# First attention layer reordered: second and third step exchanged, gMLP weight loads held until the last x rows are transposed, one row transpose per attention tile, three row blocks' output projections a step later

## The chip, the cores and the metric

One core of one Trainium2 chip. The metric is the device time of one execution in microseconds (us). The span that a profile shows is some 1.75 us shorter than the time of the same run.

## The reference, cut to what matters

```python
def reference(A_x, A_wqkv, A_wo, B_x, B_w_in, B_w_sp, B_b_sp, B_w_out):
    x = A_x                                            # (1, 2048, 576), bf16
    x = x + _A_ref(_layernorm(x), A_wqkv, A_wo)        # 32 heads of 18; each query sees 8 keys,
    x = x + _B_ref(_layernorm(x), B_w_in, B_w_sp, ...) #   2 positions apart
    x = x + _A_ref(_layernorm(x), A_wqkv, A_wo)        # B is a gMLP: w_in (576 x 4608), gelu,
    x = x + _B_ref(_layernorm(x), B_w_in, B_w_sp, ...) #   w_sp (2048 x 2048) over the rows, w_out
    return x
```

The change touches the first line of these four alone. The first attention layer takes about 135 of 1190 us.

## The kernel before

An attention layer goes through NT = 19 tiles of 112 queries, each in two steps: step 2t has heads 0 to 15 of tile t, step 2t+1 heads 16 to 31. A step is 16 logit matmuls (`L_mm`, TensorE), two exponentials (`EXP`, ScalarE) and 16 small matmuls with v (`PV`, TensorE), whose result VectorE divides by its sum (`rec`, `o_t`). All other work of the layer hangs in a table at a step number: projections of q and k (`PG`) and v (`VW`), the output projection of 128 rows (`WO`), the load of their residual (`XO`), the store of the new x (`XST`), its normalisation, and the transpose of the normalised row block for the next layer (`LN_T`). Transposes of attention rows (`o_t` to `oT`) and of row blocks are DMAs that SyncE's queue (SPq) issues in program order, together with the loads and stores.

```python
        def XO(i):                                     # two row blocks at once, on SPq
            if i % 2 == 0:
                xo = ...
                self.dma(xo[:], x_prev[i * P:(i + 2) * P, :]..., eng=nc.sync)
        def WO(i, hh):
            ...
            for c in range(5):
                nc.tensor.matmul(pw[:, 0:288], lhsT=oT[:, c, r0:r0 + P], rhs=wo_sb[:, c, hh * 288:(hh + 1) * 288], ...)
            nc.vector.tensor_tensor(out=st["x"][:, hs], in0=pw[:, 0:288], in1=st["xo"][:, hs], op=ALU.add)
        ...
        for t in range(nvw, NT):                       # nvw = 9 in the first layer
            for hh in range(2):
                if li == 0 and t == nvw:
                    at(13 * hh, VW, t, hh, True)
                else:
                    at(2 * t - 2 + hh, VW, t, hh, 2 * t - 2 + hh >= PG_END and hh == 0)
        for i in range(NS):                            # 16 row blocks
            t = -(-(i + 1) * P // QT) - 1              # the last tile that block i needs
            s = 2 * t + (6 if li == 0 and t < 10 else 5 if t < NT - 5 else 4 if t < NT - 3 else 3)
            at(s - 5, XO, i)
            at(s, WO, i, 0)
            at(s + 1, WO, i, 1)
            at(s + 1, LN_STATS, i)
            at(s + 2, LN_XN, i)
            at(s + 2, XST, i)
            if i < NS - 1:
                at(max(s + 4, 24 + (5 * i) // 4) if li == 0 else s + 4, LN_T, i)
        if li == 0:
            at(0, self.load_wo, nc.sync)
            for f in reversed(self.load_win2a(nc.gpsimd)):
                at(0, f)
        # [cut: loads of win2b, the first six PG with L_mm(0), EXP(0) and the four window fills]
        for s in range(NST):                           # NST = 38
            if s + 1 < NST:
                L_mm(s + 1)
                EXP(s + 1)
            PV(s)
            for f, a in table.pop(s, []):
                f(*a)
```

Four PSUM buffers (128 x 512) are shared by all of `PG`, `VW`, `PV` and `WO`. TensorE can start one of these only when VectorE or ScalarE has emptied the buffer of four before.

The softmax here doesn't subtract the row's maximum and nothing guards it: scores larger than these inputs give would overflow.

## Time and profile before

Three runs before the prediction gave 1190.21 us (1190.11 to 1192.29). The profile lines that carry the argument are in the prediction. This table gives what one profiled run of the kernel before shows, in us; a row of it is the start of the first instruction of that kind on TensorE.

| milestone | profile before |
|---|---|
| first PV (step 0) | 49.01 |
| PV of step 14 | 80.95 |
| PV of step 16 to PV of step 22 | 12.24 |
| PV of step 23 to PV of step 24 | 1.86 |
| last PV (step 37) | 129.18 |
| first gMLP matmul that uses the second part of its weights | 133.46 |
| end of the last matmul | 1187.78 |
| tail: from the start of VectorE's last add (1187.81) to the end | 2.99 |
| span | 1190.8 |

### The profile page before, as it was taken

Reading aid. Unit: us, or ns where it says so; the run is one execution under the profiler, and the core shown is the slowest. Engines: PE = TensorE matmul, PEld = TensorE weight load, DVE = VectorE, ACT = ScalarE, POOL = GpSimd, SP = SyncE. Lnnn points to the kernel's source line nnn. Section 1 sums busy time; section 2 is a strip of 40 time slices with the busy share of each in tenths; the row PEclk is TensorE's granted clock in tenths of the full one; section 3 lists DMA queues with packets and bytes.
Section 4 is the critical chain, followed back from the end, with each engine's and each line's share of the span. In section 5 each row is a group of like instructions: output and inputs, shape, how many; then the busy total and the mean of one; then the engine's idle time right before and its main releaser. Section 6 shows DMA issues by size and latency. Waiting matters only on the chain.

```text
span 1190.8 us, 20761 instructions
## 1 busy us (share of the span) xinstructions
PE 1180.2 (99%) x8554; PEld 620.6 (52%) x8554; DVE 547.4 (46%) x1206; ACT 376.6 (32%) x593; POOL 281.5 (24%) x383
## 2 busy tenths in 40 slices
PE   8999999999999999999999999999999999999998
PEld 5567544444444444457755775444444444444677
DVE  8688587333233233245556786753233233233311
ACT  5578677210110110202156786760110110111000
POOL 4768685000000000001153877530000000000000
PEclk9999999999999999999999999999999999999999
DMA  8989992000000000049645999900000000000332
GB/s 195 200 163 199 181 224 65 23 4 9 12 12 12 12 1 11 12 139 291 169 98 117 203 227 196 202 14 9 12 12 1 12 12 12 12 1 28 125 105 73
DMA packets 178104, 101.21 MB, mean 85 GB/s; under 512 B 134336, under 2 KB 159360, under 8 KB 178009
## 3 DMA queue, kind: packets, MB, share of 16 engines
q1 hardware_dynamic: 165144, 78.13, 30.6%
q0 software_dynamic: 6512, 16.00, 5.4%
q10 hardware_dynamic: 6352, 5.75, 1.6%
q8 instruction: 67, 1.10, 0.4%
q14 instruction: 29, 0.23, 0.1%
HBM read 42.39 MB, written 16.53 MB: 49 GB/s over the span
## 4 chain that ended last, share of the span: by engine, by line
PE 94%; DMA 3%; POOL 1%; ACT 0%; issue 0%; SPq 0%; DVE 0%; ACTq 0%; DVEq 0%
PE pg L887 42%; PE pz L869 12%; PE po L941 12%; PE pz L791 11%; PE pp L402 5%; PE pw L494 3%; PE O_ps L457 3%; PE pv L379 3%; PE L_ps L437 2%; DMA oT<-o_t 2%; PE pzs L791 1%; DMA QK<-win2a 1%; POOL QK L77 1%; DMA wqk_sb<-in_A_wqkv_dram 1%; ACT P_sb L446 0%
## 5 line engine op out<-in xcount | busy, mean ns | idle before, releaser
L887 PE MATMUL pg<-Wq,Z 128*128 128x512 bf16 x2304 | 502.8, 379 | 0.0
L887 PEld LDWEIGHTS <-Z 128*128 128x128 bf16 x2304 | 225.3, 98 | 272.0
L891 DVE TENSOR_TENSOR g_tmp<-pg,ln_xn 128x512 f32<-128x512 f32 x144 | 99.6, 692 | 429.2 <-PE pg L887 429.2
L881 ACT ACTIVATE z1T<-pz 128x1024 bf16<-128x1024 f32 x72 | 73.7, 1024 | 513.8 <-PE pz L869 513.6
L77 POOL DMA_DIRECT2D wout<-in_B_w_out_dram x4 | 4.3, 1064 | 604.6 <-PE pg L887 604.6
L941 PE MATMUL po<-wout,Z 128*128 128x288 bf16 x1152 | 141.4, 286 | 0.0
L446 ACT ACTIVATE P_sb<-L_ps 128x896 bf16<-128x896 f32 (+1 forms) x152 | 126.7, 887 | 41.2 <-PE L_ps L437 40.6
L869 PE MATMUL pz<-xnT,w 128*128 128x512 bf16 (+1 forms) x640 | 136.0, 380 | 0.0
L941 PEld LDWEIGHTS <-Z 128*128 128x128 bf16 x1152 | 112.7, 98 | 28.8
L791 PEld LDWEIGHTS <-xnT 128*128 128x128 bf16 (+1 forms) x800 | 66.2, 97 | 81.0 <-issue 23.7
L791 PE MATMUL pz<-win2a,xnT 128*128 128x512 bf16 x384 | 104.8, 380 | 0.0
L892 DVE TENSOR_TENSOR Z<-g_tmp,z1T 128x512 bf16<-128x512 f32 x144 | 99.6, 692 | 9.7
L869 PEld LDWEIGHTS <-w 128*128 128x128 bf16 (+1 forms) x640 | 51.1, 97 | 80.0 <-issue 27.1
L402 PE MATMUL pp<-xnT,wqk_sb 128*128 128x512 bf16 x360 | 83.8, 382 | 0.5 <-DMA wqk_sb<-in_A_wqkv_dram 0.5
L805 ACT ACTIVATE zp<-pz 128x1024 bf16<-128x1024 f32 x64 | 65.5, 1024 | 36.6 <-PE pz L791 32.8
L951 DVE TENSOR_TENSOR x_new<-po,xo 128x288 f32<-128x288 f32 (+1 forms) x64 | 28.8, 455 | 87.6 <-PE po L941 83.5
L791 PE MATMUL pz<-win2b,xnT 128*128 128x512 bf16 (+1 forms) x256 | 65.7, 380 | 0.0
L807 DVE CUSTOM_DVE_ANT_0 Z<-zp 128x1536 bf16<-128x1536 bf16 x32 | 56.6, 1769 | 13.1 <-ACT zp L805 13.0
L77 POOL DMA_DIRECT2D QK<-stg x81 | 50.7, 631 | 36.3 <-DVE stg L371 21.0
L379 PE MATMUL pv<-wv_sb,xnT 128*128 128x288 bf16 (+1 forms) x380 | 55.8, 285 | 0.0
L242 POOL TENSOR_SCALAR ln_xn<-x_new,ln_mv,ln_rstd 128x576 bf16<-128x576 f32 x23 | 52.8, 2294 | 2.0
L402 PEld LDWEIGHTS <-wqk_sb 128*128 128x128 bf16 x360 | 33.2, 98 | 37.2 <-DMA wqk_sb<-in_A_wqkv_dram 1.0
(114 smaller groups left out, 916.9 us busy)
## 6 DMA issues: line engine op xcount, KB each, us to landing
xres<-x_new SPq DMA_DIRECT2D x48, 288.0 KB
xo<-xres SPq DMA_DIRECT2D x32, 288.0 KB
wout<-in_B_w_out_dram POOLq DMA_DIRECT2D x4, 1296.0 KB, 8.5
xo<-xres SPq DMA_DIRECT2D x8, 576.0 KB
w<-in_B_w_in_dram SPq DMA_DIRECT2D x16, 256.0 KB
QK<-stg POOLq DMA_DIRECT2D x53, 72.0 KB, 4.4
QK<-stg SPq DMA_DIRECT2D x41, 72.0 KB
xo<-in_A_x_dram SPq DMA_DIRECT2D x8, 288.0 KB
```

The lines of the kernel that those rows point to most:

```text
L77: return eng.dma_start(out=out, in_=in_)
L379: nc.tensor.matmul(pv[:nk, 0:288], lhsT=self.xnT[:, c, QT * t:QT * t + nk], rhs=wv_sb[:, c, hh * 288:(hh + 1) * 288], start=(c == 0), stop ...
L402: nc.tensor.matmul(pp[:, :], lhsT=w, rhs=self.xnT[:, c, PADL + cc * 512:PADL + (cc + 1) * 512], start=(c == 0), stop=(c == 4))
L446: nc.scalar.activation(out=P_bufs[(2 * s + jp) % 4][:nk, :, :, 0:nq], in_=Lv[:nk, :, :, 0:nq], func=ACT.Exp, scale=scale)
L791: nc.tensor.matmul(pzvs[ci][:, sub * 512:sub * 512 + w], lhsT=self.xnT[r0:r1, c, PADL + i * P:PADL + (i + 1) * P], rhs=win2(c)[r0:r1, c0 + ...
L805: nc.scalar.activation(out=zp[:, c0:c0 + cn], in_=pzvs[ci][:, 0:cn], func=ACT.Gelu_apprx_tanh, accum_out=sums[:, ci:ci + 1])
L869: nc.tensor.matmul(pz1s[q // 2][:, q % 2, :], lhsT=w1[r0:r1, c, sub * P:(sub + 1) * P], rhs=self.xnT[r0:r1, c, PADL + q * 512:PADL + (q + ...
L881: nc.scalar.activation(out=z1T[:, q2 * 512:(q2 + 2) * 512], in_=pz1s[q2 // 2][:, :, :].rearrange("p a b -> p (a b)"), func=ACT.Gelu_apprx_ ...
L887: nc.tensor.matmul(pg[:, :], lhsT=Z[:, jj, i, sub * P:(sub + 1) * P], rhs=Wq[q][:, i, :], start=(i == 0), stop=(i == NS - 1))
L891: nc.vector.tensor_tensor(out=tmp[:], in0=pg[:, :], in1=bsp[:, qs], op=ALU.add)
L892: nc.vector.tensor_tensor(out=uT(jj)[:, sub, qs], in0=tmp[:], in1=z1Ts[jj, sub][:, qs], op=ALU.mult)
L941: nc.tensor.matmul(acc[hh], lhsT=uT(j // 2)[:, j % 2, i * P:(i + 1) * P], rhs=wouts[j // NJH][:, j % NJH, hh * 288:(hh + 1) * 288], start= ...
```

## The change

Its intent is to remove three holes of TensorE in the first attention layer: the wait for the q weights at 14 us, the wait for staged q and k rows at 48 us, and the waits for transposed attention rows near the end of the layer.

```diff
+        parts = dict(k=(D, 512, D + 64), q=(0, D, 0), q0=(0, 256, 0), q1=(256, D - 256, 256), k1=(D + 512, 64, D))
-            self.load_wqk(nc.sync)
+            self.load_wqk(nc.sync, ("k", "q0", "q1", "k1"))
 # [cut]
+        seq = list(range(NST))
+        if li == 0:
+            seq[1:3] = 2, 1
+        pbi = {s: 2 * k_ for k_, s in enumerate(seq)}      # which P_sb buffer a step uses
 # [cut: EXP and PV use pbi[s]; L_mm, EXP and PV are called with seq[s]]
-                xn = stgs[(2 + k_) % NSTG]...
+                xn = stgs[(1 + k_) % NSTG]...
 # [cut: v evacuations of tiles 4 and 5 on ScalarE; VW(9, 0) moved ahead of the loop]
                 if li == 0 and t == nvw:
-                    at(13 * hh, VW, t, hh, True)
+                    if hh == 1:
+                        at(0, VW, t, hh, True)
 # [cut]
-            s = 2 * t + (6 if li == 0 and t < 10 else 5 if ...)
+            s = 2 * t + (7 if li == 0 and 5 <= t <= 7 else 6 if li == 0 and t < 10 else 5 if ...)
 # [cut]
-                at(max(s + 4, 24 + (5 * i) // 4) if li == 0 else s + 4, LN_T, i)
+                at(s + 4 if li > 0 or i > 12 else 19 + 2 * i if i < 8 else 35 + (i - 8) // 2, LN_T, i)
         if li == 0:
+            at(1, self.fill_window_rows, QK, 1, ((4, 0),))     # two of four fills; the others before the loop
+            at(2, self.fill_window_rows, QK, 1, ((4, 1),))
             at(0, self.load_wo, nc.sync)
-            for f in reversed(self.load_win2a(nc.gpsimd)):
-                at(0, f)
+            at(0, lambda: nc.gpsimd.tensor_copy(out=rstds[:, 0:1], in_=self.xnT[:, 0, PADL + S - 1:PADL + S]))
+            w2l = self.load_win2a(nc.gpsimd)
+            for k_ in (3, 5, 4, 2, 1, 0):
+                at(0, w2l[k_])
```

The copy of one element of xnT on GpSimd is the hold: GpSimd issues the weight loads after it, and it waits for the last transposed x rows. `5 <= t <= 7` selects row blocks 4, 5 and 6.

## The prediction

> **What bounds the kernel now.** I read the page first, then the waits of TensorE (PE), then the order of time of PE, VectorE (DVE) and SyncE's DMA queue (SPq) around the holes that the waits named. The page:
>
> ```profile
> span 1190.8 us, 20761 instructions
> PE 1180.2 (99%) x8554; PEld 620.6 (52%) x8554; DVE 547.4 (46%) x1206; ACT 376.6 (32%) x593; POOL 281.5 (24%) x383
> ```
>
> PE is busy 1180.2 of 1190.8 us and carries 94% of the chain that ended last. The change touches only the first attention layer (everything in it hangs on li == 0, or has the old default), adds no matmul and removes none: the order of PE in the changed kernel has the same 17110 rows, with a few groups moved. So the whole prize is the idle and the stretched time of PE in the first 135 us; from there to the end PE is fed by itself, and what is won at 135 us should arrive at the end unchanged. The waits of PE over the whole run:
>
> ```profile
> PE pw L494 <- DMA oT<-o_t: 1.8, 2, 1.2
> PE L_ps L437 <- ACT P_sb L446: 1.6, 5, 0.4
> PE warm L541 <- POOL ident L184: 1.5, 1, 1.5
> PE pt L574 <- DVE ln_xn L567: 1.2, 2, 0.8
> PE L_ps L437 <- DMA QK<-win2a: 0.7, 1, 0.7
> PE pp L402 <- DMA wqk_sb<-in_A_wqkv_dram: 0.5, 1, 0.5
> ```
>
> Columns: total us, times, longest. The rows named DMA (oT, QK, wqk_sb) are what the change aims at: 3.0 us, 0.25% of the run. Three holes, in order of time. First, 0.55 us at 14.47 us before the first q projection, until its weights land. Second, the second logits step (tile 0, heads 16 to 31):
>
> ```profile
> 47.28 0.89 PE L437 MATMUL L_ps<-QK 32*128 32x112 bf16 x15
> 48.86 0.22 PE L437 MATMUL L_ps<-QK 32*128 32x112 bf16 x1 [0.69 <-DMA QK<-win2a]
> 49.01 0.56 PE L457 MATMUL O_ps<-v_ext,P_sb 128*128 128x19 bf16 x16
> ```
>
> Such a group of 16 takes 0.40 us where nothing holds it (57.45 us); here 47.28 to 49.01, 1.73 us, so about 1.3 us are lost, more than the wait counts. Just after it, the chain that ended last shows the same projection group at two speeds:
>
> ```profile
> 51.05 2.14 PE pp L402 x5
> ...
> 54.22 1.09 PE pp L402 x5
> ```
>
> The granted clock is 0.50 in every slice between 50.9 and 53.6 us, 1.00 before 50.5 and after 54. A window of about 3.4 us at half speed follows the hole. Its cost is 1.05 us in that group, about 1.2 us in all. Third, the end of the layer: output projections wait for transposed attention rows.
>
> ```profile
> 125.22 0.79 PE L494 MATMUL pw<-wo_sb,oT 128*128 128x288 bf16 x5 [0.59 <-DMA oT<-o_t]
> ...
> 131.51 1.39 PE L494 MATMUL pw<-wo_sb,oT 128*128 128x288 bf16 x10 [1.23 <-DMA oT<-o_t]
> ```
>
> SPq shows why: it takes some 1.23 us to issue each transpose, in order.
>
> ```profile
> 121.02 1.78 SPq L469 DMA_TRANSPOSE oT<-o_t  x1
> 122.90 1.23 SPq L249 DMA_TRANSPOSE xnT<-stg  x1
> 124.18 0.57 SPq L77 DMA_DIRECT2D xres<-x_new  x1
> 124.84 1.23 SPq L249 DMA_TRANSPOSE xnT<-stg  x1
> 126.17 0.53 SPq L77 DMA_DIRECT2D xo<-in_A_x_dram  x1
> 126.80 1.19 SPq L469 DMA_TRANSPOSE oT<-o_t  x1
> ```
>
> The transpose issued at 126.80 belongs to attention tile 16, whose rows DVE had finished at 125.3 us at the latest (the multiply at 124.85, 0.46 us). It lands 4.57 us after its issue, at 131.4. Two row transposes and one load of the residual stand between it and the one before.
>
> **What the Trainium skill says.** "TensorE: Matmul & The Clock Gate", part 1 (the HAM clock gate): PE's clock falls to half after an idle window of about 3.4 us on a free-running grid, and returns after a busy one. The trace agrees in length and ratio (0.50 for about 3.4 us, 2.14 against 1.09 us); that the free-running phase decides whether it strikes is my reason for not counting on this gain in every run. The same page (table at its top) says that VectorE is strict FIFO; so fills queued ahead of a reciprocal delay it, which matters below. The trace fits: the reciprocal at 49.61 comes after four fills that end at 49.32. "Trainium Kernel Development and Optimization", key constraints: DMAs from SP, ACT and POOL share the same 16 engines. The trace agrees: while POOL's weight loads run, 50 to 55 us, 372 GB/s move, against 143 in the next 5 us.
>
> **The change part by part.**
>
> *Weights of q in two pieces.* Before the first q group, 576+72 = 648 KB had to land after k; now 256+32 = 288 KB. At the 288 to 310 GB/s measured between 5 and 15 us, 360 KB less is about 1.2 us earlier, which covers the 0.55 us. PE is then back to back until 47 us. The two extra issues on SPq (about 0.55 us each) delay later x loads by 1.1 us, but no PE work before 39 us uses those, and DVE has 2.8 us of slack at 34.7. Gain 0.5 us.
>
> *Second and third step exchanged.* PE now has a v projection (moved ahead, 0.61 us), the logits of tile 1 heads 0 to 15 (whose rows are long in place), the first PV (0.42 us) and another v projection (formerly at step 13, 0.61 us) before it needs the late heads. Starting at 47.28 that is about 49.3, past the 48.8 landing: the DMA wait goes. But another takes its place: the two logits buffers are held by the two exponentials, 1.73 us for the pair. Logits of tile 1 end at 48.2, their exponentials at about 50.0, so the exchanged step cannot finish before about 50.2 and the next PV starts at 50.3; before, the PV in that place started at 50.46. Gain 0.2 us there, and one v projection already done. Step 13 loses that projection: its PV-to-PV time was 78.73 to 80.95, 2.22 us; steps 14 to 17, without one, average (88.31-80.95)/4 = 1.84 us, which is ScalarE's floor of two exponentials. Gain 0.38. Together 0.6 us, not 1.3.
>
> *Half-rate window.* The hole before it now holds work, so it should mostly go: 1.2 us in the profiled run. But timed runs before were 1190.11, 1190.21 and 1192.29, the profiled one 1192.6; perhaps the faster ones never had it. I count 0.5 us of the median.
>
> *gMLP weight loads held.* Six loads of 288 KB, issued at 45.99 to 51.06 while the last four x transposes (issued 41.93 to 47.13) are in flight, now wait for these. With the rest ahead of its time by some 0.7 us, the projection at step 1 needs these rows at about 50.2; holding keeps them from being late. They end on POOL about 4 us later, and POOL's first staging copy (56.40 before) is late by about 1 us at most; its columns are wanted only at step 18. Gain 0, as protection.
>
> *Window fills split.* DVE had four fills in a row (4.64 us). Two now come before the first reciprocal, one each after steps 1 and 2. DVE work in these steps is 0.26+0.46+0.69+1.16 = 2.57 us against about 2.0 for PE; four PSUM buffers carry the lag of about 1 to 2 us. Gain 0. Four v evacuations moved to ScalarE fall in its idle stretch (6.94 us before 41.78): 0.
>
> *One row transpose per tile; output projections of rows 4 to 6 one step later.* Row transposes start at step 19 and come every second step; before, from step 24, nearly every step. An attention tile then costs SPq 1.23+1.23+0.57+0.55/2 = 3.3 us, against about 4.3 us for two steps: SPq keeps up. Between the last two attention transposes one row transpose goes (1.2 us), and the residual load that stood last in front of tile 16 comes earlier (up to 0.5 us). Both oT waits (0.59+1.23 = 1.8 us) should shrink to near nothing. Gain 1.5 us.
>
> Sum: 0.5 + 0.6 + 0.5 + 1.5 = 3.1 us; 1190.2 - 3.1 = 1187.1 us.
>
> **Rivals.** (1) *The transposes only move their congestion.* For: DMA is near saturation at 85 to 135 us (SP's queue takes 94.5% of 16 engines), and the attention transpose issued at 90.38 took 9.51 us; DVE waited 1.6 us for it to reuse an output row buffer. Three more row transposes now fall between steps 19 and 23. Against: the residual stores of rows 4 to 6 move later, and SPq idles from 98 to 101.5. If so, the 1.5 us shrink to 0 and the time is about 1188.7. (2) *ScalarE floor or DVE lag eats the exchange.* With nothing from the exchange and 0.5 us lost to the fills, about 1188.2. (3) *The hole, or the half-rate window, was worth more:* the window gone in all runs, 1.2 instead of 0.5, and oT waits fully gone: about 1186.
>
> **Range and chances.** All rivals lie between 1186 and 1189; a slow run as the median could add 2 us. Range 1185.0 to 1189.8. A 2% move is 24 us, and all PE idle of the layer is about 6.5 us, so faster by over 2% is near impossible; slower by 2% would need a new stall of 20 us, and nothing in the order of instructions makes one: 0.005 each, within 2% 0.99.
>
> **What would show it.** Right: no wait of pp on wqk_sb; no wait of L_ps on QK, but the first logits steps waiting on the exponentials; clock 1.00 at 50 to 55 us; no or smaller oT waits at the end, with the last attention transpose issued within 1 us of its rows; first gMLP matmuls some 3 us earlier. Wrong: pp waiting for xnT around 50 us, DVE waiting on oT<-o_t for over 2 us at 90 to 105, or new PE idle at steps 13 to 16.

## The result, and the profile after

Four runs of the changed kernel gave a median of 1192.49 us (1191.05 to 1195.34), beside 1190.28 us for the kernel before (four runs, 1190.11 to 1192.29). The ratio is 1.0018, with a 95% interval of 0.9994 to 1.0041: within 2%, and above the predicted range of 1185.0 to 1189.8. All ratios here are those on record, of fast runs of the same rounds; they are not quite the ratios of the medians, nor of the plain means (e11: 1190.88 over 1191.54 us is 0.9994, where 1.0001 is on record).

The page of the changed kernel: the span is longer by 1.1 us, and TensorE is busy for 0.4 us more (1180.6 after 1180.2), though it does the same 8554 counted instructions.

```profile
span 1191.9 us, 20761 instructions
...
PE 1180.6 (99%) x8554; PEld 620.7 (52%) x8554; DVE 546.0 (46%) x1202; ACT 377.9 (32%) x597; POOL 275.8 (23%) x384
```

The waits of TensorE in the changed kernel (total us, times, longest): the wait on QK is gone, those on oT fell from 1.8 to 0.4, and exponentials took over, 2.5 instead of 1.6. The wait of pp on the q weights is gone, and a wait of pp on xnT has come (at 23.65 us, not near 50 us, where the prediction would have taken it as a sign of being wrong).

```profile
PE L_ps L441 <- ACT P_sb L450: 2.5, 7, 0.4
...
PE pp L402 <- DMA xnT<-ln_xn: 0.7, 1, 0.7
PE pw L498 <- DMA oT<-o_t: 0.4, 1, 0.4
```

TensorE in order of time at the exchanged steps, changed kernel (start, duration, instructions, in brackets the idle time before and what ended it). The logits at 48.18 take 0.40 us, unhindered; the first PV is at 48.51 (49.01 before). The half group at 50.37 waits for an exponential, and the second PV comes 2.16 us after the first.

```profile
48.18 0.40 PE L441 MATMUL L_ps<-QK 32*128 32x112 bf16 x16
48.51 0.57 PE L461 MATMUL O_ps<-v_ext,P_sb 128*128 128x19 bf16 x16
...
50.37 0.37 PE L441 MATMUL L_ps<-QK 32*128 32x112 bf16 x8 [0.34 <-ACT P_sb L450]
50.67 0.56 PE L461 MATMUL O_ps<-v_ext,P_sb 128*128 128x19 bf16 x16
```

So the front of the layer goes roughly as forecast: the PV of step 14 starts at 79.88, 1.07 us before its time in the profile before. But steps 16 to 22 then take 13.17 us instead of 12.24, the last PV is 0.3 us later than before, and the gMLP milestone is only 1.07 us earlier, where some 3 had been forecast. VectorE in the changed kernel shows what is new there: the add of an output projection waits 3.04 us for its residual load `xo`, and the reciprocal behind it, which empties a PSUM buffer, waits with it.

```profile
85.44 0.46 DVE L468 TENSOR_TENSOR o_t<-O_ps,rec 112x288 bf16<-112x288 f32 x1 [0.83 <-DMA oT<-o_t]
...
89.61 0.46 DVE L501 TENSOR_TENSOR x_new<-pw,xo 128x288 f32<-128x288 f32 x1 [3.04 <-DMA xo<-in_A_x_dram]
89.98 0.25 DVE L467 RECIPROCAL rec<-O_ps 112x16 f32<-112x16 f32 x1
```

SyncE's queue in the changed kernel shows why it is late: the load of xo stands behind four staging copies, which take 3.98 us to issue, and goes out at 84.96.

```profile
79.05 1.27 SPq L473 DMA_TRANSPOSE oT<-o_t  x1
80.42 3.98 SPq L77 DMA_DIRECT2D QK<-stg  x4
84.45 0.47 SPq L77 DMA_DIRECT2D xres<-x_new  x1
84.96 0.42 SPq L77 DMA_DIRECT2D xo<-in_A_x_dram  x1
```

Two more things cost time. From 86.3 to 89.7 us, and again at 687 us in the second attention layer, which the change does not touch, the profile shows TensorE at half clock. The windows view of the second one (stretch, its length, busy time and count of PE, PEld, DVE, ACT and POOL, granted clock, DMA share, GB/s):

```profile
687.00:690.40 3.40, 3.40 (x47) 2.03 (x44) 1.17 (x3) 1.64 (x4) 1.33 (x3) 0.50 1.17 267
```

And the tail, from the start of the last add to the end of the program, takes 3.77 us instead of 2.99. (The span is printed to 0.1 us, so a tail is good to 0.05.)

### The profile page after: what moved, and what is told of

It reads as the page before. It is cut to its first block, busy times and chain, and to the rows that moved or that the text cites. A ratio compares the mean times of both kernels' runs of the same rounds, so it can differ in the third digit from the quotient of the medians.

```text
span 1191.9 us, 20761 instructions
## 1 busy us (share of the span) xinstructions
PE 1180.6 (99%) x8554; PEld 620.7 (52%) x8554; DVE 546.0 (46%) x1202; ACT 377.9 (32%) x597; POOL 275.8 (23%) x384
## 3 DMA queue, kind: packets, MB, share of 16 engines
q10 hardware_dynamic: 6352, 5.75, 1.6%
## 4 chain that ended last, share of the span: by engine, by line
PE 96%; DMA 2%; ACT 1%; issue 0%; SPq 0%; DVE 0%; ACTq 0%
PE pg L896 42%; PE pz L878 12%; PE po L950 12%; PE pz L800 11%; PE pp L402 6%; PE pv L379 3%; PE pw L498 3%; PE O_ps L461 3%; PE L_ps L441 2%; PE pzs L800 1%; ACT P_sb L450 1%; DMA wqk_sb<-in_A_wqkv_dram 1%; DMA oT<-o_t 1%; DMA oT<-in_A_x_dram 0%; SPq L77 0%
```

## The experiments

Three candidates were on the table for the missing 3 us: the later output projections of row blocks 4 to 6 (with the late residual load), half-clock windows that strike elsewhere, and the longer end of the program; and a fourth, that the one profile of the kernel before had been a poor base. Milestones of the profiles, in us, in the columns of the table above and three more, PV of step 16 to PV of step 22, PV of step 23 to PV of step 24, and the tail, from the start of VectorE's last add to the end (row "before" is that profile again; "clock 1.0" marks a profiled run whose mean granted clock was 1.0):

| profile | first PV | step 14 | 16 to 22 | 23 to 24 | step 37 | gMLP | end PE | tail | span |
|---|---|---|---|---|---|---|---|---|---|
| before | 49.01 | 80.95 | 12.24 | 1.86 | 129.18 | 133.46 | 1187.78 | 2.99 | 1190.8 |
| e5, before again (clock 1.0) | 48.74 | 79.71 | 12.25 | 1.62 | 127.21 | 131.50 | 1185.84 | 3.03 | 1188.9 |
| e6, before again | 50.39 | 84.75 | 12.24 | 1.62 | 132.64 | 137.38 | 1191.70 | 3.06 | 1194.8 |
| after | 48.51 | 79.88 | 13.17 | 2.06 | 129.50 | 132.39 | 1188.09 | 3.77 | 1191.9 |
| e1, after again (clock 1.0) | 47.48 | 78.85 | 12.93 | 2.06 | 127.68 | 130.56 | 1184.88 | 3.78 | 1188.7 |
| e13, after again | 47.35 | 78.72 | 15.22 | 2.06 | 130.24 | 133.12 | 1187.44 | 3.73 | 1191.2 |
| e16, after again | 47.93 | 79.31 | 13.68 | 2.06 | 128.90 | 131.78 | 1188.52 | 3.74 | 1192.3 |
| e2, projections undone (clock 1.0) | 47.94 | 80.52 | 12.25 | 1.62 | 128.07 | 130.96 | 1185.28 | 3.38 | 1188.7 |
| e3, row transposes undone | 47.55 | 79.27 | 13.00 | 2.07 | 128.18 | 133.40 | 1188.93 | 3.74 | 1192.7 |
| e4, idle matmuls added (clock 1.0) | 47.62 | 78.99 | 14.27 | 2.21 | 129.53 | 132.42 | 1188.44 | 3.72 | 1192.2 |
| e7, residual load earlier | 47.79 | 79.17 | 14.11 | 2.19 | 129.19 | 132.08 | 1187.52 | 3.74 | 1191.3 |
| e8, q in one load | 47.58 | 78.96 | 14.02 | 2.19 | 128.88 | 131.76 | 1186.52 | 3.04 | 1189.6 |
| e9, no exchange | 49.13 | 80.87 | 14.46 | 2.21 | 131.24 | 134.13 | 1188.88 | 3.79 | 1192.7 |
| e10, no hold | 47.25 | 83.10 | 11.82 | 2.17 | 130.82 | 133.70 | 1188.02 | 3.74 | 1191.8 |
| e11, e2 and e8 together (clock 1.0) | 47.24 | 78.61 | 12.24 | 1.61 | 126.16 | 129.04 | 1183.36 | 3.01 | 1186.4 |
| e12, e11 and v projection back | 47.36 | 79.37 | 15.34 | 1.62 | 130.03 | 132.92 | 1187.23 | 3.03 | 1190.3 |
| e14, before and later projections | 48.33 | 79.91 | 13.55 | 2.22 | 129.10 | 132.39 | 1186.70 | 3.06 | 1189.8 |
| e15, e11 again | 47.66 | 79.02 | 14.85 | 1.62 | 129.18 | 132.07 | 1187.79 | 2.97 | 1190.8 |

And the times, each beside the kernel before on the same chip and in the same rounds. A call, in what follows, is one submission of several runs to one chip: e1 to e4; e5 and e6; e7 to e10; e11 to e14; e15 and e16. The last column counts the runs whose mean granted clock was 1.0 as listed, not 0.999 or less.

| run | n | median us | ratio to before, 95% | clock 1.0 |
|---|---|---|---|---|
| after | 4 | 1192.49 | 1.0018 [0.9994, 1.0041] | 0 |
| e1 (after) | 6 | 1191.87 | 1.0001 [0.9982, 1.0019] | 2 |
| e13 (after) | 6 | 1191.22 | 1.0000 [0.9983, 1.0016] | 1 |
| e16 (after) | 6 | 1192.36 | 0.9995 [0.9974, 1.0015] | 0 |
| e5 (before) | 6 | 1192.59 | 1.0005 [0.9982, 1.0027] | 2 |
| e2 | 6 | 1191.63 | 0.9995 [0.9977, 1.0013] | 3 |
| e3 | 6 | 1193.05 | 1.0013 [0.9994, 1.0032] | 1 |
| e4 | 6 | 1194.09 | 1.0014 [0.9998, 1.0030] | 4 |
| e7 | 5 | 1191.77 | 1.0010 [0.9998, 1.0023] | 1 |
| e8 | 5 | 1191.32 | 1.0001 [0.9988, 1.0013] | 1 |
| e9 | 5 | 1194.45 | 1.0024 [1.0011, 1.0038] | 0 |
| e10 | 5 | 1193.67 | 1.0030 [1.0017, 1.0044] | 0 |
| e11 | 6 | 1190.09 | 1.0001 [0.9979, 1.0022] | 3 |
| e12 | 6 | 1191.20 | 1.0003 [0.9982, 1.0024] | 2 |
| e14 | 6 | 1192.48 | 1.0012 [0.9992, 1.0031] | 2 |
| e15 | 6 | 1191.17 | 0.9988 [0.9968, 1.0009] | 2 |

### The two kernels unedited: e1, e13, e16 (after) and e5, e6 (before)

No edit: the same kernels were run several times because single runs of one differ by more than the effect.

> The changed kernel again, unedited. Theory CHANCE (the number of half-rate windows of TensorE differs from run to run by the phase of a free-running grid; the first four runs of the changed kernel were unlucky): median at or below 1190.3, ratio to before 0.998 to 1.000. Theory PLACE (the change thins TensorE's work at attention steps 13 to 16 and so makes a half-rate window there in nearly every run, 1.3 us): median again 1191 to 1194, and the profile again shows a granted clock well under 1.00 between 80 and 95 us. Theory TRANSPOSES (row transposes in steps 19 to 23 slow the chain): waits for oT or o_t longer than in the first profile.

> The kernel before, unedited, submitted as a run to get a second profile of it. Reason: in the call before, five of its eleven runs had a granted clock of 1.0 and took 1189.96 to 1191.44 us, no longer than the changed kernel's runs at 1.0. Theory ATYPICAL (the profile that the prediction was read from was a run with a bad hole at 47 us and a half-rate window after it; in most runs of the kernel before these are smaller or absent, so there was less to win): in this profile, if its clock is 1.0, the second logits group starts its PV before 48.5 us, the first gMLP matmuls with win2b come at 130.5 to 131.5 instead of 133.46, and the waits for oT are under 1 us. Theory GIVEN BACK (the kernel before always has the hole and the waits; the changed kernel wins them in the first layer and loses as much later): the hole at 47 us and the win2b matmuls at 132.5 to 133.5 come again, and the end is no later than the changed kernel's only because later stages are shorter.

> The kernel before once more, one look, for a third profile. ATYPICAL and GIVEN BACK as for the run before it; and the spread of the start of the first gMLP matmuls over three profiles shows how far one profile can be trusted: CHANCE expects it to differ by 1.5 us or more between profiles of the same kernel.

> The changed kernel, unedited, as the partner of the others in this call. PLACE: at most two of six runs at clock 1.0, a window at 80 to 95 us in the profile with a chance of about 5 in 7 (five of seven profiles of kernels with the thinned steps and no filler had it). Median 1191.5 to 1192.5.

> The changed kernel as its partner. GIVEN BACK BY THE LATER PROJECTIONS: steps 16 to 22 take 12.9 us or more (12.93, 13.17 and 15.22 in its three profiles so far), step 24 2.06 us, tail 3.75 us, median 0.5 to 2 us above the run beside it. CHANCE: no difference beyond 0.7 us.

Of what was expected: e1 bore out neither CHANCE (its median is above 1190.3) nor PLACE (its profile has no window at 80 to 95 us). e5 met one of ATYPICAL's three signs (gMLP at 131.50; but its first PV is at 48.74 and its oT wait 1.5 us). e6 met CHANCE, with a spread of 5.9 us. e13 met PLACE (one run at clock 1.0, a window at 90 us), with a median 0.3 us under the range. e16 met what was expected of it, but the intervals of both e15 and e16 hold 1.

The 60 runs of the kernel before in the experiments (e5 and e6 among them) have a mean of 1192.10 us, a median of 1191.72 and a standard deviation of 2.10. The 22 runs of the changed kernel (the first four, e1, e13 and e16) have a mean of 1192.19 and a median of 1192.09. So the change is worth nothing that these runs can see: a mean difference of +0.1 us, with a standard error of about 0.4 (0.27 and 0.34, added in squares). The base of the prediction, 1190.21 us, was a lucky draw of three.

The spread has a visible part. Of the 60 runs before, 24 had a mean clock of 1.0, and those average 1190.30 us; of the 22 runs after, 3 had it (1190.76 us). With different chips and rounds mixed in, 24 of 60 against 3 of 22 speaks for half-clock windows striking the changed kernel more often; the count over all runs, after e14 below, says the same more clearly.

The three profiles of the kernel before differ by 5.9 us at the start of the gMLP (131.50 to 137.38). The one that I predicted from had a half-clock window at 50 us and two oT waits; e5, at full clock, has the hole at 48 us, one oT wait of 1.5 us and no window; e6 has three oT waits (4.0 us in all) and a half-clock window at 76 to 79.5 us, just after the first of them (1.61 us). The waits of TensorE in e5:

```profile
PE L_ps L437 <- ACT P_sb L446: 1.6, 5, 0.4
PE pw L494 <- DMA oT<-o_t: 1.5, 1, 1.5
...
PE L_ps L437 <- DMA QK<-win2a: 0.7, 2, 0.5
```

There is no wait of pp for wqk_sb among them: that one is 0.55 us in the first profile of before, 0.40 in e6, 0 in e5.

e5 and e1 are the two kernels at full clock, so they give the cleanest ledger, worked out from the table. To the PV of step 16 (83.39 in e5, 82.52 in e1) the changed kernel gains 0.87 us; from step 16 to 22 it gives back 0.68; from 22 to 37 it gives back 0.66; at the end of the layer it gains 1.41. The sum, 0.94 us gained at the start of the gMLP (131.50 to 130.56), is still there at TensorE's end (0.96, 1185.84 to 1184.88). Then the tail takes 0.75 us of it back: 0.2 us of span remain.

SyncE's queue in e5, to be held against that of the changed kernel above: here xo is issued at 79.31, ahead of the staging copies.

```profile
77.94 1.26 SPq L469 DMA_TRANSPOSE oT<-o_t  x1
79.31 0.52 SPq L77 DMA_DIRECT2D xo<-in_A_x_dram  x1
79.92 3.10 SPq L77 DMA_DIRECT2D QK<-stg  x4
```

In e1 it goes out at 83.81. VectorE waits 1.36 us for it there, then 1.48 us for an o_t buffer that a late transpose still reads, and TensorE has a wait that no profile of the kernel before has:

```profile
PE pv L379 <- DVE o_t L468: 1.1, 1, 1.1
```

Which of VectorE's two waits holds TensorE? The chain that ended last (start, duration) goes through the transpose in e1:

```profile
84.34 4.55 DMA oT<-o_t
```

and through the load in e16:

```profile
84.63 4.84 DMA xo<-in_A_x_dram
```

It is the load in e13 and e4 too, where TensorE waits 1.83 and 1.14 us for the add that needs it (1.64 in e16), and the transpose in e3 and e14. The two are issued one directly after the other, behind the same four staging copies (83.81 and 84.34 in e1). So what stalls is that place in the queue; the price of the load alone is not separated from that of the transpose.

Steps 16 to 22 took 12.24 to 12.25 us in all three profiles of the kernel before, and 12.93 to 15.22 in all four of the changed one.

### e2: later output projections undone

```diff
-            s = 2 * t + (7 if li == 0 and 5 <= t <= 7 else 6 if li == 0 and t < 10 else ...)
+            s = 2 * t + (6 if li == 0 and t < 10 else ...)
```

> The changed kernel with the output projections of rows 4 to 6 back at their old steps (16 to 21), so step 16 has its projection again and steps 22 and 23 lose it. PLACE: the half-rate window between 80 and 95 us is gone or rarer, and the time falls by about 1.3 us against the changed kernel of the same call; CHANCE: no difference clear of 1 us; TRANSPOSES: no difference, or slower because the stores come a step earlier.

In the profile, steps 16 to 22 are back at 12.25 us and step 23 to 24 at 1.62; no wait for xo is left. The time is 1191.63 us against 1191.87 for e1 of the same call: no difference to be seen. Waits for oT came back instead (0.33 and 0.52 us, at 66 and 72 us), and the gain to step 14 was lost with them (80.52). From step 16 to 37 it takes 43.88 us, against 45.16 in e1 and 43.82 in e5.

### e3: row transposes back in their old places

```diff
-                at(s + 4 if li > 0 or i > 12 else 19 + 2 * i if i < 8 else 35 + (i - 8) // 2, LN_T, i)
+                at(max(s + 4, 24 + (5 * i) // 4) if li == 0 else s + 4, LN_T, i)
```

> The changed kernel with the old schedule of row transposes (none before step 24, then nearly every step). If spreading them is what saves the waits for oT at the end of the layer, those waits come back: 1 to 1.8 us more, first gMLP matmuls behind the output projections that much later. TRANSPOSES: faster than the changed kernel by 1 us or more. PLACE and CHANCE: slower by 0.5 to 1.8 us.

The oT wait is back: 2.1 us in all in e3, 0 in e1. TensorE in order of time, e3:

```profile
131.19 1.39 PE L498 MATMUL pw<-wo_sb,oT 128*128 128x288 bf16 x10 [1.92 <-DMA oT<-o_t]
```

The first gMLP matmul comes 2.8 us later than in e1, more than the wait, because a half-clock window falls into 131 to 136 us. The time is 1193.05 us, 1.2 us above e1 of the same call; the interval still holds 1. So this part of the change works in the profile, with about the size forecast; the time doesn't resolve it.

### e4: idle matmuls to keep TensorE busy in steps 13 to 17

```diff
+        NJ_ = {13: 4, 14: 4, 15: 4, 16: 8, 17: 4} if li == 0 else {}
+            for _ in range(NJ_.get(s, 0)):      # into columns of O_ps that nobody reads
+                nc.tensor.matmul(O_ps[:, 16 * (DH + 1):512], lhsT=wo_sb[:, 0, 0:P], rhs=wo_sb[:, 0, 0:512 - 16 * (DH + 1)], ...)
```

> The changed kernel with 24 idle matmuls of 208 columns (4 in each of steps 13, 14, 15, 17 and 8 in step 16 of the first attention), written to unused columns of a PSUM tile: about 0.09 us each, in time that TensorE waits for ScalarE anyway. PLACE: no half-rate window at 80 to 95 us, time 1 to 1.5 us less than the changed kernel of this call. CHANCE: no difference beyond 0.5 us, or up to 0.5 us slower. If the matmuls are not free, up to 2 us slower, with longer steps 13 to 17.

Four of six runs had clock 1.0, more than any other changed kernel, and the profile has no window; yet the time is 1194.09 us, the highest of that call. The wait for xo (3.03 us) is still there without any window, and so is the long stretch of 14.27 us from step 16 to 22. The stall and the window are thus two things, and PLACE's gain in time did not come.

### e7: the residual load one step earlier, projections left late

```diff
-            at(s - 5, XO, i)
+            at(s - (6 if li == 0 and 5 <= t <= 7 else 5), XO, i)
```

> The changed kernel, but the residual loads of rows 4 to 7 are issued one step earlier, at the steps they had before (the later output projections had dragged them along, behind four staging copies on SyncE's queue). Theory XO (this dragged load is what stalls VectorE, and through PSUM TensorE, at steps 18 to 20 of the changed kernel: waits of 1.4 and 3.0 us for xo in its two profiles): no wait of x_new for xo over 0.5 us, steps 18 to 20 take 2.1 to 2.2 us each instead of one of 3.2, the first gMLP matmuls with win2b come at 129.3 to 130.0 us in a profile with clock 1.0 (130.56 in the changed kernel's), median about 1 us below the changed kernel's 1191.87 to 1192.49. Rival REUSE (the wait for the transposes of o_t is what stalls, whatever the residual load does): the stall at steps 19 to 20 stays at 1 us or more.

The wait for xo is gone, and steps 16 to 22 still take 14.11 us, at 1191.77 us. But this doesn't decide between XO and REUSE: a half-clock window lies on just these steps, from 84.1 to 90.9 us (e8, with a window in the same place and a wait of 3.5 us for xo, takes 14.02), and the transpose behind the copies is issued no earlier than in e1 (84.91 against 84.34). REUSE stays open. Windows view of e7:

```profile
81.00:84.00 3.00, 2.46 (x59) 1.71 (x56) 2.33 (x8) 3.00 (x5) 2.83 (x4) 1.00 1.00 74
84.00:85.00 1.00, 0.84 (x21) 0.67 (x21) 0.01 (x1) 1.00 (x3) 1.00 (x1) 0.54 0.86 207
85.00:88.00 3.00, 3.00 (x50) 1.92 (x47) 1.86 (x6) 1.66 (x3) 2.83 (x4) 0.50 0.94 249
```

In the 3 us before the clock fell, TensorE was busy for 2.46 us by the profile. It was not idle, but had only logits and PV groups to do, at ScalarE's pace: ScalarE is busy for 3.00 of 3.00 us. e4 and e7 together show that the stall occurs without the window, and the window without the wait for xo.

### e8: the q weights in one load again

```diff
-            self.load_wqk(nc.sync, ("k", "q0", "q1", "k1"))
+            self.load_wqk(nc.sync)
```

> The changed kernel with the q weights in one load again. My prediction: a wait of pp on wqk_sb of 0.4 to 0.6 us comes back at 14 us, everything after it 0.3 to 0.5 us later. Rival: two of the three profiles of the kernel before have no such wait to speak of in the end (the first logits came at 40.90 in one, 41.31 and 42.96 in the others; 40.57 and 41.60 in the changed kernel), so no difference beyond 0.2 us. SyncE's program is two instructions shorter: if the late instruction fetch at the end (0.75 us) hangs on its length, it goes and the tail from the last add to the end is 3.0 instead of 3.75 us.

Two findings. TensorE does not wait for the q weights in this profile either, and the PV of step 14 starts at 78.96, as early as with the split (78.72 to 79.88): the split buys nothing here. And the tail is 3.04 us instead of 3.75. The time (1191.32 us, ratio 1.0001) doesn't tell it from the changed kernel.

### e9: steps not exchanged, v projections in their old places

```diff
-        if li == 0:
-            seq[1:3] = 2, 1
-                    if hh == 1:
-                        at(0, VW, t, hh, True)
+                    at(13 * hh, VW, t, hh, True)
-            VW(nvw, 0, True)          # ahead of the loop
```

> The changed kernel without the exchange (steps in order, the two v projections of tile 9 back at steps 0 and 13). My prediction: the first PV comes about 1.2 us later (48.6 to 49.0 instead of 47.5), and 0.6 us of it is left at the end of the layer. CHANCE: a half-rate window near 50 us is likelier.

The wait for staged rows is back. TensorE in order of time, e9:

```profile
48.98 0.22 PE L439 MATMUL L_ps<-QK 32*128 32x112 bf16 x1 [0.35 <-DMA QK<-win2a]
49.13 0.56 PE L459 MATMUL O_ps<-v_ext,P_sb 128*128 128x19 bf16 x16
```

The first PV is at 49.13 (47.35 to 48.51 in the four changed profiles), and the time, 1194.45 us, is 0.24% above the kernel before, with an interval that leaves out 1. The changed kernel itself was between 0.9995 and 1.0018 in its calls, so the exchange is worth about 2 us here; that comparison goes across calls and chips, so its size is rough. In its own call, e7 and e8, which have the exchange, average 1192.10 and 1190.98 us, and e9 1193.91. It is not less than I had forecast.

### e10: no hold, weight loads issued at once

```diff
-            at(0, lambda: nc.gpsimd.tensor_copy(out=rstds[:, 0:1], in_=self.xnT[:, 0, PADL + S - 1:PADL + S]))
-            for k_ in (3, 5, 4, 2, 1, 0):
+            for k_ in (5, 4, 3, 2, 1, 0):
```

> The changed kernel with the gMLP weight loads not held and in the old order. My prediction: no gain from holding beyond protection, so 0 to 0.5 us slower, the loss, if any, as a wait of pp for xnT near 50 us. Rival: POOL's waiting behind the held loads costs; then faster by up to 0.5 us.

TensorE in order of time, e10: after the first PVs a q/k projection stands for 2.95 us.

```profile
49.41 0.56 PE L461 MATMUL O_ps<-v_ext,P_sb 128*128 128x19 bf16 x16
52.93 0.57 PE L402 MATMUL pp<-xnT,wqk_sb 128*128 128x512 bf16 x1 [2.95 <-issue]
...
55.66 0.60 PE L461 MATMUL O_ps<-v_ext,P_sb 128*128 128x19 bf16 x16
```

The releaser is given as "issue", that is, none that the profile shows; the matmul reads the xnT rows whose transposes this edit lets the weight loads overtake. That it waits for these is the likeliest reading, and no more. One step takes 6.25 us, and the time is 0.30% above the kernel before [0.17%, 0.44%], far more than the 0 to 0.5 us that I had expected. The changed kernel needs the hold. Why the kernel before does without it is open: there the same projection starts at 50.90 without a wait, and the transposes are issued no earlier (from 41.93 us; 41.73 in e10), but the first weight loads 1.45 us later (45.99; 44.54).

e10 also shows, unintended, the later projections without the stall, as TensorE comes to step 16 some 4 us later and VectorE waits neither for xo nor for an o_t buffer. From step 16 to 37 it takes 44.05 us. Its steps 16 to 19 and 22 to 25 take just what e1's take (5.36 and 6.34 us); the difference lies between 19 and 22 (6.46 against 7.57).

### e11, e15: e2 and e8 together; e12: also VW(9, 1) back at step 13

```diff
 # e11 and e15: the diffs of e2 and e8.  e12: those, and
-                        at(0, VW, t, hh, True)
+                        at(13, VW, t, hh, True)
```

> The changed kernel with the output projections of rows 4 to 6 back at steps 16 to 21 and the q weights in one load. PLACE (thinned steps 13 to 17 draw a half-rate window at 80 to 95 us) with TAIL (the late instruction fetch costs 0.75 us): no window at 80 to 95 us, tail 3.0 to 3.4 us, three or more of six runs at clock 1.0, median 1 to 2 us below the changed kernel of this call and 0.5 to 1.5 us below the kernel before. CHANCE: within 0.7 us of both.

> The same, and the second v projection of tile 9 back at step 13, so that steps 13 to 17 hold what they held before the change. PLACE: clock 1.0 at least as often as in the run without this, the first layer ends at most 0.3 us later in a profile of equal clock. If the exchange needs that projection as filler at step 0: no difference there, because the exponentials bind (first to second PV 2.16 us either way).

> The changed kernel with the later output projections undone and q in one load (e11) once more, because its profile was 2.5 us below the kernel before's of equal clock and its median 2.3 us, but one slow run left the interval wide. Theory GIVEN BACK BY THE LATER PROJECTIONS: steps 16 to 22 take 12.2 to 12.3 us again, step 24 1.6 us, tail 3.0 us, and the mean of its twelve runs is 1 us or more below the kernel before. CHANCE: the mean of the twelve is within 0.7 us of the kernel before.

The profile of e11, at full clock, is what the prediction had described. Against e5 it gains 1.11 us to step 16, loses nothing from 16 to 22 (12.24 us) and 0.07 to step 37, gains 1.41 at the end and keeps its tail (3.01): 2.5 us of span, 1188.9 to 1186.4. It is the shortest span of any profile here, and its time of 1188.18 us the lowest of any edited kernel. Held against e1, also at full clock, it prices the later projections (the two differ in these and in the q load). From the PV of step 16 to that of 19, e1 takes 5.36 us and e11 5.73: with one output projection less there, 0.37 us are won. From 19 to 22, 7.57 against 6.51: 1.06 lost, the stall. From 22 to 25, 6.34 against 5.75 (5.80 in e5): 0.59 lost, because the last of the moved matmuls now lies in step 22, which had only a v projection; its step time goes to 2.22 us, and the next one can't be 1.61 any more but is 2.06. Moving the matmuls alone thus costs 0.2 us (as in e10, without the stall), and the stall 1.1.

But the gain doesn't hold in every run. In e15, the same kernel, an output projection of the restored order meets a transpose that is not there yet, and a half-clock window follows. TensorE in order of time, e15:

```profile
84.83 0.79 PE L498 MATMUL pw<-wo_sb,oT 128*128 128x288 bf16 x5 [1.58 <-DMA oT<-o_t]
```

e12 has the same wait, 2.2 us. The early front of the layer may bring TensorE to these projections sooner than SyncE's queue brings the transposed rows, which is presumably why the change put them a step later; but e6, the kernel before with its late front, waits 1.61 us for such rows as well, at 75 us. Ratios of 1.0001 and 0.9988, both intervals over 1: e11 is no proven improvement. The 12 runs of e11 and e15 have a mean of 1191.17 us (standard error 0.63) against 1192.10 for the kernel before, which falls between the two theories. e12 has clock 1.0 less often than e11 (2 against 3 of six runs), against PLACE.

### e14: the kernel before, with later projections and both v projections at step 0

```diff
-                    at(13 * hh, VW, t, hh, True)
+                    at(0, VW, t, hh, True)
-            s = 2 * t + (6 if li == 0 and t < 10 else ...)
+            s = 2 * t + (7 if li == 0 and 5 <= t <= 7 else 6 if li == 0 and t < 10 else ...)
```

> The kernel before with the thinning alone: output projections of rows 4 to 6 one step later, the second v projection of tile 9 at step 0 instead of 13. PLACE: a half-rate window at 80 to 95 us in the profile, fewer runs at clock 1.0 than the kernel before (14 of 37 so far), median 1 us or more above it. CHANCE: no difference beyond 0.7 us, runs at clock 1.0 as often as before.

The kernel before now shows the same damage in the same place: a wait of 1.44 us for xo, 13.55 us from step 16 to 22, 2.22 us from 23 to 24, and a half-clock window at 86 to 89.4. Its time, 1192.48 us, is 0.12% above the kernel before, with an interval that holds 1, and its median 0.1 us above, not the 1 us of PLACE. That these two moves bring the stall is shown; its price in the mean isn't resolved.

Over all profiles, a wait of over 1.3 us for xo occurs in eight of the ten that have the later projections with the load at s - 5 (after, e1, e3, e4, e8, e13, e14, e16; not e9 and e10, which reach step 14 later than the changed kernel, at 80.87 and 83.10), and in none of the seven that have the old place (the largest there is 0.42 us). e7 has the load at its old step and no wait.

The half-clock windows of the first layer can be counted in the same way. There are 13 in the 18 profiles. Seven open within 1.7 us of a hole of TensorE: 0.69 us in the first profile of before, 1.61 in e6, 2.95 in e10, 2.16 in e12, 1.83 in e13, 1.58 in e15, 1.92 ahead of e3's second. The other six (after, e3, e7, e8, e9, e14) open 1.1 to 2.7 us after the PV of step 16, with no wait over 0.5 us ahead of them. These six are among the ten profiles that have the later projections and no filler; none of the seven with the projections in their old place has such a one, nor e4 with its filler. Step 16 is the one that the later projections leave with logits and PV alone. The runs say the same: with later projections and no filler, 8 of 54 have clock 1.0; with the old place, 34 of 84. Neither a hole nor a thin step draws a window every time: e16 has none after its hole of 1.64 us, e1 none after its thin step 16. In the traces, the stretch from the first full clock to such a window is a whole multiple of 3.413 us (44.37, 78.51, 81.92 us), on a grid whose place in the span differs from run to run; that this grid decides which ones strike is not shown.

### The tail

In the kernel before, the last 2 us of the profile hold nothing but the store of the output. DMA in the last 2 us, before:

```profile
q10 hardware_dynamic: 144, 0.07, 11.9%
```

In the changed kernel the same stretch holds one instruction fetch of 0.01 MB, and the store lies ahead of it:

```profile
q14 instruction: 1, 0.01, 1.1%
```

The tail was 2.99 to 3.06 us in the three profiles of before and in e8, e11, e12, e14 and e15, and 3.72 to 3.79 us in the four of the changed kernel and in e3, e4, e7, e9 and e10; e2 has 3.38. All nine of the second group have the q weights in two loads, and a fetch within the last 2 us; all eight of the first have one load, and no fetch there. e2, with two loads, has none there either, and a store that ends later. Why a load more at 10 us moves the last fetch of instructions stays open; no run here settles it.

## Why the prediction was wrong

**The base.** I took 1190.2 us from three runs. The mean of 60 is 1192.1 with a standard deviation of 2.1, so a prediction of the median of a few runs had to have at least that spread, and the range of 1185.0 to 1189.8 lay below it. Some 1.5 us of the miss (the pooled median 1191.72 less 1190.2) is this, and no step of the mechanism. The profile that I read was of a worse run than the timed ones: at full clock the kernel before starts its gMLP at 131.5, not 133.5.

**Weights of q in two pieces, 0.5 us: wrong.** The wait isn't there in every run (0.55, 0.40 and 0 us in three profiles of before; 0 with one load in e8), and the 0.75 us of tail goes with the split in every profile but e2's 3.38. On SPq the prediction saw no harm, as no work of TensorE before 39 us needs the x loads behind the two extra issues. But transposes of x rows stand there too: in the first profile after, they are issued from 14.76 us instead of 14.34, right behind the x loads, and TensorE waits 0.66 us for transposed rows at 23.65. The nine other profiles with the split have no such wait.

**Exchange, 0.6 us: right in kind and about in size, but one of its two terms failed.** The hole at 48 us is filled, the exponentials bind in its place, and the second PV starts at 50.67 where I had computed 50.3. Of the 0.87 us in the ledger to step 16, 0.33 are there at the first logits already (40.90 in e5, 40.57 in e1), although e5 has no q wait to lose; 0.26 of these arise in the v projections at 33 us, whose evacuations moved (5.32 and 5.06 us). So the exchange itself gives some 0.5 us, all of it by step 2. The 0.38 forecast at step 13 did not come: the lead is 0.86 us before it and 0.87 at step 16, for without its v projection step 13 takes the same 2.22 us, and TensorE waits 0.42 us there for an exponential. e9 shows the exchange to be worth at least its 0.6.

**Half-rate window, 0.5 us: wrong.** It left 50 us (but for e10) and came back at 84 to 95 in most profiles (after, e3, e7, e8, e9, e13), and clock 1.0 became no more frequent (3 of 22 runs against 24 of 60). I had tied the window to one hole and didn't ask what the change does to the rest of the layer. By the count after e14, windows follow holes of 0.69 to 2.95 us, or step 16, which the later projections make thin. The Trainium skill, "TensorE: Matmul & The Clock Gate", section "A second HAM failure mode: psum-queue depth-cycling", describes a clock that swings because of many short pauses, which fits the windows after a thin step (2.46 us of busy TensorE in the 3 us ahead of e7's) better than the idle window of part 1, from which I argued; but the page has a clock that swings again and again, and here a profile shows none, one or two such stretches. That the later projections draw these windows rests on the count, not on a run in which nothing else differs, and why they strike in one run and not in the next isn't shown.

**Hold, 0 us: right as protection,** and it protects from some 3 us (e10). That run is also the better sign for the 16 shared engines that the prediction cites: its own pair, 372 against 143 GB/s, shows only that more was moved.

**Fills and v evacuations, 0 us:** nothing in the profiles speaks against it; no run tested it by itself. The reciprocal at 49.61, which the prediction gives as a sign that fills delay one, doesn't show it: the fills end at 49.32, and it waits the last 0.29 us for TensorE.

**One row transpose per tile, 1.5 us: right.** The oT waits at the end were 1.8, 1.5 and (e6) 2.4 us before and 0.4, 0, 0 and 0 after; 1.41 us in the ledger; back with e3. The rival that the congestion only moves came true in part: VectorE did wait, at 84 to 90 us, for the residual load, which I hadn't named, and in e1 for an o_t buffer (1.48 us), which I had. The row transposes are not its cause: e3, which has them back in their old places, has both waits (1.45 and 1.43 us).

**Output projections of rows 4 to 6 one step later, no cost: this is the step that failed.** I had put these into the same heading as the row transposes and given them no line in the sum. They cost twice. Their matmuls leave step 16 for step 22, which lets TensorE follow ScalarE closely at first (0.37 us won) and makes it the bound later (0.59 us lost). And, which is most of it, TensorE then runs into SyncE's queue: `XO` is at s - 5, so the load moves a step later, where four staging copies stand ahead of it, and is issued at 83.81 to 84.96 us (79.31 in e5), with the next transpose of attention rows right behind it. VectorE waits 1.4 to 3.7 us for the load, or last for the o_t buffer of that transpose. VectorE takes its instructions strictly in order (the same page, the table at its top; the trace agrees: the reciprocal at 89.98 follows the add at 89.61 that had waited), so PSUM and o_t buffers stay occupied and TensorE stands, for 1.06 us in e1. Together this is 1.28 us, e1 against e11, or 1.34 us from step 16 to 37 against e5: a term that I had at 0. That the later projections bring this stall is shown; whether the load or the transpose behind it would have to be cured is open, because of e7's window. Undone together with the q split, the forecast gain appears in one full-clock profile (e11: 2.5 us of span). Undone, however, they wait for oT in two of four profiles (e12 2.2, e15 1.6 us). So moving them isn't a blunder but a trade of one wait for another, and which is cheaper in the mean these runs can't say.

**The tail, not foreseen:** 0.75 us.

In the full-clock ledger the sum reads: 0.87 + 1.41 gained, 1.34 and 0.75 given back, 0.2 us left, where I had 3.1. Two slips of the prediction change nothing: its 17110 rows of TensorE are 17108 by its page (twice 8554), and its first rival's 1188.7 should be 1188.6 (1190.2 less 1.6). What stays open: which of load and transpose holds TensorE, the share of the half-clock windows in the mean, and what decides the last instruction fetch.

## What to carry to other kernels

Before forecasting a gain of 0.3%, take several profiles of the kernel before and size each hole from the one at full clock: holes and half-clock windows that come and go aren't there to be won in every run. When a piece of work moves by a step, follow everything scheduled relative to it (here its load, which fell behind four other issues in the same queue), and ask which engine bounds the step that it leaves and the one that it enters. Compare the last 4 us too: 0.75 us more of tail can undo a hole closed a thousand us earlier.

## What the Trainium skill lacked or had wrong

- "TensorE: Matmul & The Clock Gate", part 1 and "The abstract rule" of its section "HAM oscillation": they ask for no idle gaps of some 3.4 us. Here the clock was 0.50 for about 3.4 us with no such gap: after waits of 0.69 to 2.95 us, and after none over 0.5 us, with TensorE busy for 2.46 of the 3 us ahead of it in e7. The section on the second failure mode has the nearer case but gives no measure of how thin is too thin. One such window costs 1.05 us in a group of five 128x512 matmuls (2.14 against 1.09 us).
- The same page says that the phase varies from run to run but gives no spread of run times to plan with. Here the same kernel, 60 runs, has a standard deviation of 2.10 us at 1192.10 us; the runs with clock 1.0 (24 of 60) average 1190.30.
- No page tells of an instruction fetch as the last thing in a program (it would belong to "Runtime: NRT & Kernel Launch", "Instruction fetch mechanics"): the tail was 3.0 us without it and 3.75 with it, but for e2's 3.38 without.
- "DMA: Bandwidth & Descriptors" has no time measured on this chip for what a transfer issued on SyncE's queue costs those behind it. Here a transpose of attention rows took 1.2 to 2.7 us to issue, four staging copies 3.07 to 4.1 us, and a residual load behind them went out at 83.81 to 84.96 us, against 79.31 and 80.38 ahead of them.
